# Attention over learned memories and a cosine feed-forward layer on one core: part-array products in longer pieces, and the whole turns of the cosine written as integers

## The chip, the cores and the metric

The kernel runs on one core of a Trainium2 chip. The metric is the device time of one execution in microseconds (us). Before the change the median of three runs is 718.47 us (717.94 to 719.61). A core has five engines that work side by side, each with its own queue of instructions: PE (TensorE, matrix products, results into PSUM), DVE (VectorE), ACT (ScalarE), POOL (GpSimd) and SP (which here issues most of the loads and stores). PE's weight loads are shown as an engine of their own, PEld.

## The reference

Eight batches of eight heads, 576 tokens, head size 64, 32 memories per head; then a feed-forward layer with 512 inputs and 2048 hidden units.

```python
a = phi - np.max(phi, axis=2, keepdims=True)
a = np.exp(a)
a = a / (np.sum(a, axis=2, keepdims=True) + 1e-09)
k_m = np.einsum('bhsm,bhsd->bhmd', a, k)
v_m = np.einsum('bhsm,bhsd->bhmd', a, v)
scores = scale * np.matmul(q, k_m.transpose(0, 1, 3, 2))
...
attn = attn / (np.sum(attn, axis=-1, keepdims=True) + 1e-09)
attn_out = np.matmul(attn, v_m)
...
h = x @ w_in          # x is attn_out, 4608 tokens x 512
g = h * np.cos(h)
return g @ w_out
```

Per batch and head, softmax weights over the tokens build 32 memory keys and values; each token then attends to the 32 memories, and the result goes through the layer with `h * cos(h)`. Weights arrive as 8-byte numbers and are brought to float32 and then to pairs of float16 (a high part and a rest) on the chip.

## The kernel before

**Two kinds of work.** The main loop runs over `12 * 16` units: twelve groups of 384 tokens (`grp`), each with sixteen slices of 128 hidden units (`f`). One unit is a first GEMM into a PSUM bank `hp` (`gemm1`, L500; in float32 for group 0, L491), the cosine on ACT and DVE (`act`, `act_end`), and a second GEMM that adds into three output accumulators (`gemm2`, L544; L539 for group 0). The second GEMM runs four units behind (`LAG`). A group of 384 tokens is two thirds of a batch or two halves: groups 1, 4, 7 and 10 hold the end of one batch and the beginning of the next, so `regions` gives two regions of 192 columns, the others one of 384.

**The cosine of a unit** (`act`, L505; `act_end`, L518). ACT writes `u = hp * c + 0.25`, the angle in turns (L509, once for each region); DVE casts `u` to integers `ni` (L514, the cast rounds) and subtracts them (L515); ACT takes the sine of 2 pi u (L519), which is the cosine of h; DVE multiplies it with `hp` (L523; L521 in group 0); ACT and DVE split the product into two float16 parts (L525, L526). The integers lie in the buffer `gp` that later takes the product (six buffers); `u` has three.

**The fold.** The attention's last product and the first GEMM are folded: `v_m` is multiplied into `w_in` first. For each batch `b`, a quarter `q` of the hidden units and each half `g` of the heads, `fold_psum` (L428) fills one PSUM bank `pv`, and `split_fold` (L443) brings it to two float16 parts `vw` on ACT (L445) and DVE (L446). For batch 1 the products are float32 on half of PE's columns (L433); from batch 2 on they are eight float16 products, each on a quarter of the columns (L439, shown as 128*32). Batch 0 has its own path (`fold_first`, L462).

**Preparing a batch** (`prep`: `memory`, L222, then `attend`, L331) is a generator. It yields after each small step: the softmax over tokens; the k/v products (L254, 40 products in float32 on a quarter of the columns, in five chunks of tokens; one yield after each chunk) into one bank `psA`; the division and transposes; the score products (L356, float32 on half of the columns, in three blocks of 256, 256 and 64 tokens, each into its own bank, with a DVE transpose after each, L358); softmax over memories; and the float16 parts of the weights. The k/v yields stand in this loop:

```python
for c, (s0, n) in enumerate(TCH):
    for g in range(2):
        for j in range(4):
            h = 4 * g + j
            nc.tensor.matmul(psA[32 * j:32 * (j + 1), g * KV:(g + 1) * KV],
                             lhsT=a[:n, c, h * M:(h + 1) * M], rhs=kvs[c][:n, h * KV:(h + 1) * KV],
                             start=(c == 0 and g == 0), stop=(c == 4), skip_group_check=True)
    yield
```

**The order of the work.** The main loop calls a batch's steps in a stretch of units (`jobs`), at the pace of `NSTEP = 24` steps over the stretch, and issues the folds at fixed units (`folds`): one half `(q, g)` every two units. Loads of the next batch are issued by steps of the one before (`load_phi`, `load_kv` after the k/v products, `load_q` after the scores). The order written in the program is a priority: a planner orders each engine's queue from it, from its own estimates of durations and from when buffers come free, so that instructions can be issued earlier or later than they are written; only a few are pinned (`keep_in_program_order`). On the chip each queue is then worked off in that order.

**PSUM.** Eight banks: three output accumulators, three for `hp`, and a pool of two (`ps_s`, `small_ps`) that folds, k/v products, transposes and scores share.

Of the kernel before, what the change touches and what calls it, by code (L numbers as in the profile page):

```python
# [22 lines left out]
P = 128  # L23
# [12 lines left out]
BLK = [(0, 256), (256, 256), (512, 64)]  # L36
BLK_FIRST = [(0, 256), (256, GT - 256), (GT, S - GT)]
TWO_PI_BELOW = 6.283185
EXP_MASK = 0x7F800000
NT = 4  # L40
LAG = 4
# [3 lines left out]
def attention_then_ffn(ctx: ExitStack, tc: tile.TileContext, phi, phiT, kv, qT, w_in, w_out, eye, out):  # L45
# [9 lines left out]
    def small_ps(name):  # L55
        return ps_s.tile([P, 512], F32, tag="ps_s", name=name)
# [5 lines left out]
    nc.vector.memset(vmask, 0.0)  # L62
    for j in range(4):
        nc.vector.memset(vmask[32 * j:32 * (j + 1), :, (j + 1) % 2], 1.0)

    w_in_sb = const.tile([P, NP, DF], F32, name="w_in_sb")

# [153 lines left out]
    def memory(b):  # L221
        a = loads.pop(("phi", b))  # L222
        if b < NT:

            nmx = wk.tile([P, 2], F32, tag="nmx", name=f"nmx_{b}", bufs=1)
            nc.vector.tensor_reduce(out=nmx, in_=loads.pop(("phiT", b)), op=ALU.max, axis=AX.X)
            top = small_ps(f"top_{b}")[:, 0:HM]
            for g in range(2):
                nc.tensor.matmul(top[:, g * P:(g + 1) * P], lhsT=nmx[:, g:g + 1].broadcast_to([P, P]), rhs=ident,
                                 start=True, stop=True)  # L230
        else:
            top = st["top", b]
        yield
        if b >= NT:
            yield
            yield
        for c0, c1, n in ((0, 2, P), (2, 4, P), (4, 5, S - 512)) if b == 0 else ((0, 4, P), (4, 5, S - 512)):
            ins = nc.vector.tensor_tensor(out=a[:n, c0:c1], in0=a[:n, c0:c1],
                                          in1=top[:n].unsqueeze(1).broadcast_to([n, c1 - c0, HM]),
                                          op=ALU.subtract)  # L240
            if b >= NT:

                tc.keep_in_program_order(ins)
            nc.scalar.activation(a[:n, c0:c1], a[:n, c0:c1], AF.Exp)  # L244
        yield
        if b:
            yield
        kvs = loads.pop(("kv", b))
        psA = small_ps(f"psA_{b}")
# [4 lines that stand above are left out]
                    nc.tensor.matmul(  # L254
                        psA[32 * j:32 * (j + 1), g * KV:(g + 1) * KV],
                        lhsT=a[:n, c, h * M:(h + 1) * M], rhs=kvs[c][:n, h * KV:(h + 1) * KV],
                        start=(c == 0 and g == 0), stop=(c == 4), skip_group_check=True)
            yield
        if b >= 1 and b + 1 < B and b + 1 != 2:
            load_phi(b + 1)  # L260
            load_kv(b + 1)
        pv = psA[:, 0:2 * KV].rearrange("p (g x) -> p g x", g=2)
        den = wk.tile([P, 2], F32, tag="den", name=f"den_{b}")
        nc.vector.tensor_scalar(out=den, in0=pv[:, :, 2 * D], scalar1=1e-9, scalar2=None, op0=ALU.add)
        nc.vector.reciprocal(out=den, in_=den)
        X = wk.tile([P, 2, P], F32, tag="X", name=f"X_{b}", bufs=1)
        for g in range(2):
            nc.vector.tensor_scalar(out=X[:, g], in0=pv[:, g, 0:2 * D], scalar1=den[:, g:g + 1], scalar2=None,
                                    op0=ALU.mult)
        if b:  # L270
            yield
        tpx = small_ps(f"tpx_{b}")
        for g in range(2):
            nc.tensor.matmul(tpx[:, g * P:(g + 1) * P], lhsT=X[:, g], rhs=ident, start=True, stop=True)
        km = wk.tile([P, NP, 2 * M], F32, tag="km", name=f"km_{b}", bufs=1)
        vm = wk.tile([P, NP, 2 * M], F32, tag="vm", name=f"vm_{b}")
        nc.gpsimd.memset(km, 0.0)
        nc.gpsimd.memset(vm, 0.0)
        tv = tpx[:, 0:HM].rearrange("p (c t m) -> p c t m", t=2, m=M)
        lo, hi = slice(0, D), slice(D, P)  # L280
        nc.scalar.mul(km[lo, :, 0:M], tv[lo, :, 0], 1.0 / math.sqrt(D))
        nc.scalar.mul(km[hi, :, M:2 * M], tv[hi, :, 1], 1.0 / math.sqrt(D))
        nc.vector.tensor_copy(out=vm[hi, :, 0:M], in_=tv[hi, :, 0])
        nc.vector.tensor_copy(out=vm[lo, :, M:2 * M], in_=tv[lo, :, 1])
        st["km", b], st["vm", b] = km, vm
        yield
        l1 = wk.tile([P, 4], F32, tag="l1", name=f"l1_{b}")
        nc.vector.tensor_reduce(out=l1, in_=X.rearrange("p g (t d) -> p (g t) d", t=2), op=ALU.add, axis=AX.X,
                                apply_absolute_value=True)
        nc.vector.tensor_tensor(out=l1, in0=l1, in1=vmask.rearrange("p g t -> p (g t)"), op=ALU.mult)  # L290
        l2 = wk.tile([P, 1], F32, tag="l2", name=f"l2_{b}")
        nc.vector.tensor_reduce(out=l2, in_=l1, op=ALU.max, axis=AX.X)
        l3 = wk.tile([P, 1], F32, tag="l3", name=f"l3_{b}")
        nc.gpsimd.partition_all_reduce(l3, l2, channels=P, reduce_op=RED.max)
        st["l3", b] = l3
        v_scale(b)
        yield
# [33 lines left out]
    def attend(b):  # L331
# [16 lines left out]
            flatp = at[:, r.start * M:r.stop * M]  # L348
            return flatp, flatp.rearrange("p (x m) -> p x m", m=M), r, r.stop - r.start

        def scores(i):
            t0, n = BL[i]
            sc = small_ps(f"sc_{b}_{t0}")
            for g in range(2):
                for p in range(2):
                    nc.tensor.matmul(sc[D * p:D * (p + 1), g * n:(g + 1) * n], lhsT=km[:, 2 * g + p],  # L356
                                     rhs=qt[:, 2 * g + p, t0:t0 + n], start=True, stop=True)
            nc.vector.transpose(at[:, 2 * t0:2 * (t0 + n)], sc[:, :2 * n])  # L358

        def shift(blocks):  # L360
            _, v, r, n = piece(blocks)
# [26 lines left out]
        if b == 0:  # L388
# [10 lines left out]
                    back(i)  # L399
                yield  # L400
            return
        for i in range(3):
            scores(i)
            yield
        if b >= 1 and b + 1 < B and b + 1 != 2:
            load_q(b + 1)
        pieces = ((0,), (1, 2))
# [38 lines left out]
        nc.vector.scalar_tensor_tensor(out=vw[:, 1, g], in0=src, scalar=T, in1=vw[:, 0, g],  # L446
                                       op0=ALU.mult, op1=ALU.subtract)

    def fold(b, q, g):
        if g == 0:  # L450
            st["vw", b, q] = wk.tile([P, 2, 2, FS], F16, tag="vw", name=f"vw_{b}_{q}", bufs=8)
        split_fold(b, st["vw", b, q], g, fold_psum(b, q, g))

    def fold_first(j):
        q, r = divmod(j, 2)
# [21 lines left out]
    def regions(grp):  # L477
        pair, r = divmod(grp, 3)
        b0 = 2 * pair
        if r == 0:  # L480
            return [(b0, 0, 0, GT)]
        if r == 1:
            return [(b0, GT, 0, S - GT), (b0 + 1, 0, S - GT, S - GT)]
        return [(b0 + 1, S - GT, 0, GT)]
# [20 lines left out]
    def act(grp, f, hp, pin=False):  # L505
        u = ew.tile([P, GT], F32, tag="u", name=f"u_{grp}_{f}", bufs=3)
        gp = ew.tile([P, GT], F32, tag="gp", name=f"gp_{grp}_{f}", bufs=6)
        for b, t0, c0, n in regions(grp):
            ins = nc.scalar.activation(u[:, c0:c0 + n], hp[:, c0:c0 + n], AF.Copy,  # L509
                                       scale=st["cu", b] if grp else 1.0 / (2.0 * math.pi), bias=0.25)  # L510
            if pin:
                tc.keep_in_program_order(ins)
        ni = gp.bitcast(I32)
        nc.vector.tensor_copy(out=ni, in_=u)  # L514
        nc.vector.tensor_tensor(out=u, in0=u, in1=ni, op=ALU.subtract)  # L515
        return u, gp

    def act_end(grp, f, hp, u, gp):  # L518
        nc.scalar.activation(u, u, AF.Sin, scale=TWO_PI_BELOW)  # L519
        if grp == 0:  # L520
            nc.vector.tensor_tensor(out=gp, in0=hp[:, :GT], in1=u, op=ALU.mult)  # L521
            return grp, f, gp
        nc.vector.scalar_tensor_tensor(out=u, in0=hp[:, :GT], scalar=2.0 ** -17, in1=u, op0=ALU.mult, op1=ALU.mult)  # L523
        gp = gp.bitcast(F16).rearrange("p (w x) -> p w x", w=2)
        nc.scalar.copy(gp[:, 0], u)  # L525
        nc.vector.tensor_tensor(out=gp[:, 1], in0=u, in1=gp[:, 0], op=ALU.subtract)  # L526
        return grp, f, gp
# [131 lines left out]
    for b in range(1, B):  # L659
        use = 48 * (b // 2) + 16 * (b % 2)  # L660
        before, length = {1: (5, 10), 2: (5, 13), 3: (6, 16)}.get(b, (6, 17) if b % 2 else (13, 18))
        jobs.append((b, use - before - length, use - before - 1))
        for q in range(NQ):
            for g in range(2):
                folds.setdefault(use - before + 4 * q + 2 * g, []).append((b, q, g))
    gens = {}
    pending, begun = [], []
    for i in range(12 * NF):
# [19 lines left out]
            pending.append(act_end(*begun.pop(0)))  # L688
        if len(pending) > LAG:
            gemm2(*pending.pop(0))  # L690
        for b, q, g in folds.get(i, ()):
            if q == g == 0:
                scales(b)
            fold(b, q, g)
        if i % 48 in (8, 24) and i > 8:
            out_scales(2 * (i // 48) + (i % 48 == 24))
        for b, s, e in jobs:
# [57 lines left out]
```

## Time and profile before

| | before |
|---|---|
| median of 3 runs | 718.47 us (717.94 to 719.61) |
| profiled execution, span from first to last instruction | 718.6 us |
| PE busy | 696.1 us (97%), 4578 matmuls |
| DVE busy | 570.4 us (79%), 1257 instructions |
| ACT busy | 521.5 us (73%), 965 instructions |
| mean granted clock of PE | 0.988 |

The profiled execution's span, 718.6 us, stands 0.1 us above the median of the runs. In the page, a group's row gives the line, engine, operation, output and inputs, shapes and count, then the busy time in us, the mean of one in ns, and the idle time of that engine just before, with what ended it. A matmul's shape 128*32 means 128 rows and 32 columns of the array. `issue` as a releaser means that the engine waited for nothing that the profile shows. Matmuls are pipelined, so their own lengths overlap; start-to-start distances tell what each costs.

### The profile page before, as it was taken

The page shows a single profiled execution, that of the slowest core. Times are in us where ns is not written, and L with a number is a line of the kernel's source. Part 1 is how long each engine was busy: PE and PEld are TensorE (multiplying, and loading weights), DVE is VectorE, ACT ScalarE, POOL GpSimd, SP SyncE. Part 2 cuts the span into 40 slices and gives each one's busy share as a digit, 9 for nine tenths or more (in the row PEclk, how much of TensorE's full clock was granted, in tenths as well). Part 3 has the DMA queues.
Part 4 walks back from the last instruction along what each step waited for, and adds up shares of the span by engine and source line. Part 5 has one row for each costly group of instructions (what it writes and reads, how often), then busy time and mean ns, then how long its engine had stood idle before and what let it go on. Part 6 is the DMA issues. An engine that isn't in the chain of part 4 may idle for free.

```text
span 718.6 us, 12024 instructions
## 1 busy us (share of the span) xinstructions
PE 696.1 (97%) x4578; PEld 357.7 (50%) x4578; DVE 570.4 (79%) x1257; ACT 521.5 (73%) x965; POOL 14.1 (2%) x34
## 2 busy tenths in 40 slices
PE   7689999999999999999999999999999999999997
PEld 3344445455445444666444444565444544555553
DVE  2778999998998997679876897679776987676764
ACT  1689999899887875678767696678767785665652
POOL 0000000000000000000000100000000000000000
PEclk9699999999999999999999999999999999999999
DMA  9994891525505300152103310152100000100101
GB/s 291 378 326 155 278 325 42 133 60 152 163 21 167 110 1 1 45 166 67 45 1 119 90 69 1 45 167 68 44 1 1 17 29 1 45 1 1 45 0 45
DMA packets 32233, 66.78 MB, mean 93 GB/s; under 512 B 2224, under 2 KB 12336, under 8 KB 32176
## 3 DMA queue, kind: packets, MB, share of 16 engines
q1 hardware_dynamic: 27712, 58.02, 25.1%
q10 hardware_dynamic: 4464, 8.00, 2.9%
q8 instruction: 36, 0.59, 0.4%
q14 instruction: 21, 0.17, 0.1%
HBM read 52.38 MB, written 9.44 MB: 86 GB/s over the span
## 4 chain that ended last, share of the span: by engine, by line
PE 65%; ACT 16%; DVE 13%; DMA 3%; issue 2%; SPq 1%; POOL 0%; ACTq 0%; DVEq 0%
PE acc L544 37%; PE hp L500 19%; PE pv L439 3%; ACT u L519 2%; ACT u L509 2%; DVE u L515 2%; DVE u L523 2%; PE sc L356 2%; DVE gp L526 2%; PE psA L254 2%; ACT L519 1%; DMA kv<-in_kv 1%; ACT L244 1%; DVE gp L514 1%; ACT vw L445 1%
## 5 line engine op out<-in xcount | busy, mean ns | idle before, releaser
L544 PE MATMUL acc<-wo,gp 128*128 128x512 f16 x1584 | 371.2, 379 | 0.0
L544 PEld LDWEIGHTS <-gp 128*128 128x128 f16 x1584 | 153.4, 98 | 161.5 <-issue 2.6
L500 PE MATMUL hp<-aT,vw 128*128 128x192 f16 (+1 forms) x1440 | 202.6, 284 | 0.3 <-DVE u L523 0.2
L500 PEld LDWEIGHTS <-vw 128*128 128x128 f16 x1440 | 125.0, 98 | 81.5 <-issue 29.0
L519 ACT ACTIVATE u<-u 128x384 f32<-128x384 f32 x192 | 100.2, 525 | 85.0 <-DVE u L515 84.1
L523 DVE SCALAR_TENSOR_TENSOR u<-hp,u 128x384 f32<-128x384 f32 x176 | 97.0, 553 | 45.7 <-ACT u L519 43.4
L509 ACT ACTIVATE u<-hp,cu 128x192 f32<-128x192 f32 (+1 forms) x240 | 110.7, 493 | 19.5 <-PE hp L500 11.9
L526 DVE TENSOR_TENSOR gp<-u,gp 128x384 f16<-128x384 f32 x176 | 96.7, 552 | 29.8 <-ACT gp L525 29.3
L525 ACT CAST gp<-u 128x384 f16<-128x384 f32 x176 | 89.2, 510 | 39.3 <-DVE u L523 37.1
L515 DVE TENSOR_TENSOR u<-u,gp 128x384 f32<-128x384 f32 x192 | 105.8, 553 | 3.2
L514 DVE CAST gp<-u 128x384 int32<-128x384 f32 x192 | 67.5, 353 | 21.6 <-ACT u L509 20.0
L539 PE MATMUL acc<-wo,gp 128*128 128x512 f32 x96 | 45.5, 603 | 1.6 <-DVE gp L521 1.6
L446 DVE SCALAR_TENSOR_TENSOR vw<-pv,vw 128x512 f16<-128x512 f32 x48 | 33.1, 689 | 4.2 <-ACT vw L445 3.0
L445 ACT ACTIVATE vw<-pv 128x512 f16<-128x512 f32 x48 | 28.4, 591 | 6.2 <-PE pv L439 5.4
L491 PE MATMUL hp<-aT,vf 128*128 128x384 f32 x64 | 26.5, 546 | 4.7 <-DVE gp L521 2.0
L519 ACT ACT_TABLE_LOAD x23 | 29.5, 1283 | 0.4
L539 PEld LDWEIGHTS acc<-wo,gp 128*128 128x128 f32 x96 | 17.0, 190 | 20.6 <-issue 14.7
L254 PE MATMUL psA<-kv,phi 128*32 128x129 f32 (+1 forms) x640 | 24.0, 280 | 3.2 <-DMA kv<-in_kv 1.8
L568 ACT ACTIVATE ob<-acc,os 128x512 f32<-128x512 f32 x27 | 17.9, 684 | 7.5 <-PE acc L544 5.6
L254 PEld LDWEIGHTS psA<-kv,phi 128*32 128x32 f32 (+1 forms) x640 | 16.3, 110 | 13.8 <-issue 7.4
L491 PEld LDWEIGHTS hp<-aT,vf 128*128 128x128 f32 x64 | 12.5, 207 | 18.2 <-DVE gp L521 4.6
L356 PE MATMUL sc<-q,km 128*64 128x256 f32 (+3 forms) x192 | 20.1, 337 | 0.0
(128 smaller groups left out, 555.5 us busy)
## 6 DMA issues: line engine op xcount, KB each, us to landing
kv<-in_kv SPq DMA_DIRECT2D x32, 516.0 KB, 5.6
raw_out<-in_w_out SPq DMA_DIRECT2D x8, 1024.0 KB, 4.9
q<-in_qT SPq DMA_DIRECT2D x7, 1152.0 KB, 5.5
out<-ob ACTq DMA_DIRECT2D x30, 256.0 KB, 2.1
raw_in<-in_w_in SPq DMA_DIRECT2D x6, 1024.0 KB, 7.9
phi<-in_phi SPq DMA_DIRECT2D x8, 512.0 KB, 6.7
w_in_sb<-w_in_parts SPq DMA_DIRECT2D x12, 256.0 KB, 4.4
phiT<-in_phiT SPq DMA_DIRECT2D x4, 576.0 KB, 6.4
```

The source lines that it names most:

```text
L254: nc.tensor.matmul(psA[32 * j:32 * (j + 1), g * KV:(g + 1) * KV], lhsT=a[:n, c, h * M:(h + 1) * M], rhs=kvs[c][:n, h * KV:(h + 1) * KV], s ...
L491: nc.tensor.matmul(hp[:, :GT], lhsT=st["vf", q][:, g, fo * P:(fo + 1) * P], rhs=st["aTf"][:, g], start=(g == 0), stop=(g == 1))
L500: nc.tensor.matmul(hp[:, c0:c0 + n], lhsT=vw[:, wi, g, fo * P:(fo + 1) * P], rhs=aT[:, ai, g, c1:c1 + n], start=(k == 0), stop=(k == 5))
L509: ins = nc.scalar.activation(u[:, c0:c0 + n], hp[:, c0:c0 + n], AF.Copy, scale=st["cu", b] if grp else 1.0 / (2.0 * math.pi), bias=0.25)
L514: nc.vector.tensor_copy(out=ni, in_=u)
L515: nc.vector.tensor_tensor(out=u, in0=u, in1=ni, op=ALU.subtract)
L519: nc.scalar.activation(u, u, AF.Sin, scale=TWO_PI_BELOW)
L523: nc.vector.scalar_tensor_tensor(out=u, in0=hp[:, :GT], scalar=2.0 ** -17, in1=u, op0=ALU.mult, op1=ALU.mult)
L525: nc.scalar.copy(gp[:, 0], u)
L526: nc.vector.tensor_tensor(out=gp[:, 1], in0=u, in1=gp[:, 0], op=ALU.subtract)
L539: nc.tensor.matmul(accs[grp][t], lhsT=gp[:, t * P:(t + 1) * P], rhs=wo[:, f + 1], start=(f == 0), stop=(f == NF - 1))
L544: nc.tensor.matmul(accs[grp][t], lhsT=gp[:, gi, t * P:(t + 1) * P], rhs=parts[:, wi], start=(f == 0 and gi == 0 and wi == 0), stop=(f == N ...
```

## The change

- `memory`: for batches after the first, the yield after each of the five k/v chunks is dropped; one yield follows after all five.
- `attend`: for batches after the first, the products of score blocks 0 and 1 are issued one after the other, into two banks, before the transposes of both; block 2 follows as before. Two yields instead of three.
- `fold`: both halves `g` are issued in one call. Products first, for both banks, then the splits. In the main loop a fold of a quarter stands at one unit (`4 * q + 1`) instead of two (`4 * q` and `4 * q + 2`).
- `act`: ACT writes `hp * c + 0.25` straight into the integer tile `ni` (its write rounds); DVE then computes `hp * c - ni` in one instruction from PSUM, once for each region. The cast is gone. The quarter turn, which the subtraction no longer holds, goes to the sine as a bias of pi/2 from a constant tile.

```diff
+    quarter = const.tile([P, 1], F32, name="quarter")
+    nc.vector.memset(quarter, HALF_PI_BELOW)
...
                         lhsT=a[:n, c, h * M:(h + 1) * M], rhs=kvs[c][:n, h * KV:(h + 1) * KV],
                         start=(c == 0 and g == 0), stop=(c == 4), skip_group_check=True)
+            if b == 0:
+                yield
+        if b:
             yield
...
-        for i in range(3):
-            scores(i)
-            yield
+        score_products(0)
+        score_products(1)
+        score_back(0)
+        score_back(1)
+        yield
+        score_products(2)
+        score_back(2)
+        yield
...
-    def fold(b, q, g):
-        if g == 0:
-            st["vw", b, q] = wk.tile([P, 2, 2, FS], F16, tag="vw", name=f"vw_{b}_{q}", bufs=8)
-        split_fold(b, st["vw", b, q], g, fold_psum(b, q, g))
+    def fold(b, q):
+        vw = wk.tile([P, 2, 2, FS], F16, tag="vw", name=f"vw_{b}_{q}", bufs=8)
+        st["vw", b, q] = vw
+        for g, pv in enumerate([fold_psum(b, q, g) for g in range(2)]):
+            split_fold(b, vw, g, pv)
...
+        ni = gp.bitcast(I32)
         for b, t0, c0, n in regions(grp):
-            ins = nc.scalar.activation(u[:, c0:c0 + n], hp[:, c0:c0 + n], AF.Copy,
-                                       scale=st["cu", b] if grp else 1.0 / (2.0 * math.pi), bias=0.25)
+            c, cu = slice(c0, c0 + n), st["cu", b] if grp else 1.0 / (2.0 * math.pi)
+            ins = nc.scalar.activation(ni[:, c], hp[:, c], AF.Copy, scale=cu, bias=0.25)
             if pin:
                 tc.keep_in_program_order(ins)
-        ni = gp.bitcast(I32)
-        nc.vector.tensor_copy(out=ni, in_=u)
-        nc.vector.tensor_tensor(out=u, in0=u, in1=ni, op=ALU.subtract)
+            nc.vector.scalar_tensor_tensor(out=u[:, c], in0=hp[:, c], scalar=cu, in1=ni[:, c],
+                                           op0=ALU.mult, op1=ALU.subtract)
...
-        nc.scalar.activation(u, u, AF.Sin, scale=TWO_PI_BELOW)
+        nc.scalar.activation(u, u, AF.Sin, scale=TWO_PI_BELOW, bias=quarter)
...
-            for g in range(2):
-                folds.setdefault(use - before + 4 * q + 2 * g, []).append((b, q, g))
+            folds.setdefault(use - before + 4 * q + 1, []).append((b, q))
```

`score_products(i)` and `score_back(i)` are the two halves of the old `scores(i)`: its four products, and its DVE transpose.

More of the change, by code (lines that the diff above doesn't have):

```diff
@@ L38 @@
 TWO_PI_BELOW = 6.283185
+HALF_PI_BELOW = 1.5707962
 EXP_MASK = 0x7F800000
@@ L349, in piece, with score_products @@
             return flatp, flatp.rearrange("p (x m) -> p x m", m=M), r, r.stop - r.start
-        def scores(i):
+        sc_at = {}
+        def score_products(i):
             t0, n = BL[i]
-            sc = small_ps(f"sc_{b}_{t0}")
+            sc_at[i] = sc = small_ps(f"sc_{b}_{t0}")
             for g in range(2):
@@ L357, in scores, with score_back @@
                                      rhs=qt[:, 2 * g + p, t0:t0 + n], start=True, stop=True)
-            nc.vector.transpose(at[:, 2 * t0:2 * (t0 + n)], sc[:, :2 * n])
+        def score_back(i):
+            t0, n = BL[i]
+            nc.vector.transpose(at[:, 2 * t0:2 * (t0 + n)], sc_at[i][:, :2 * n])
+        def scores(i):
+            score_products(i)
+            score_back(i)
         def shift(blocks):
@@ L690, in attention_then_ffn @@
             gemm2(*pending.pop(0))
-        for b, q, g in folds.get(i, ()):
-            if q == g == 0:
+        for b, q in folds.get(i, ()):
+            if q == 0:
                 scales(b)
-            fold(b, q, g)
+            fold(b, q)
         if i % 48 in (8, 24) and i > 8:
```

## Prediction

> **What bounds the kernel now.** I read the page's engine totals first, then busy time by stretch, then TensorE's timeline around the products that the change regroups, then the waits.
>
> ```profile
> PE 696.1 (97%) x4578; PEld 357.7 (50%) x4578; DVE 570.4 (79%) x1257; ACT 521.5 (73%) x965; POOL 14.1 (2%) x34
> ...
> PEclk9699999999999999999999999999999999999999
> ```
>
> ```profile
> 72.00:108.00 36.00, 34.36 (x117) 15.34 (x118) 34.38 (x73) 35.94 (x52) 0.91 (x3) 1.00 0.88 303
> 108.00:144.00 36.00, 36.00 (x188) 17.87 (x187) 35.16 (x76) 33.24 (x69) 0.35 (x1) 1.00 0.32 85
> 144.00:180.00 36.00, 35.66 (x294) 20.84 (x294) 33.16 (x65) 33.30 (x64) 0.31 (x1) 1.00 0.41 108
> 180.00:714.00 534.00, 532.64 (x3640) 275.65 (x3639) 419.54 (x947) 370.90 (x716) 10.53 (x19) 1.00 0.16 51
> ```
>
> The columns of the second are the stretch, its length, then PE, weight loads, DVE, ACT, POOL, the clock, the DMA share. From 108 us to 714 PE is busy for 604.3 of 606 us, at full clock. DVE is idle for 114 of the last 534 us, ACT for 163. So PE sets the end from 108 us on, and there only less PE time makes the kernel shorter. Before that, ACT is full (35.94 of 36) and DVE nearly.
>
> A busy PE isn't a streaming PE, though. This is its timeline around one fold of batch 4 (start, length, engine, line):
>
> ```profile
> 431.66 2.11 PE L544 MATMUL acc<-wo,gp 128*128 128x512 f16 x9
> 433.60 1.14 PE L500 MATMUL hp<-aT,vw 128*128 128x384 f16 x6
> 434.57 2.10 PE L544 MATMUL acc<-wo,gp 128*128 128x512 f16 x9
> 436.61 0.40 PE L439 MATMUL pv<-w_in,vp 128*32 128x512 f16 x4
> 436.84 0.39 PE L439 MATMUL pv<-w_in,vl 128*32 128x512 f16 x4
> 437.16 1.15 PE L500 MATMUL hp<-aT,vw 128*128 128x384 f16 x6
> ```
>
> Nine full-array matmuls followed by full-array ones take 433.60 - 431.66 = 1.94 us, or 0.216 each. Followed by products on a quarter of the columns (128*32) they take 436.61 - 434.57 = 2.04: **0.10 us going in**. The four `vp` products run side by side in 0.23 us (436.84 - 436.61), the four `vl` ones in 0.32 before a full-array matmul starts: **0.09 us coming out**. With 0.01 more on the first matmul after it, a trip out of the full array and back costs about 0.20 us beside its work. The waits view shows the trips at the weight loads:
>
> ```profile
> PEld L500 <- issue: 29.0, 79, 0.8
> PEld L439 <- issue: 19.7, 47, 0.4
> ...
> PEld psA L254 <- issue: 7.4, 18, 1.1
> ...
> PEld sc L356 <- issue: 4.4, 11, 0.6
> ...
> PEld pv L433 <- issue: 2.2, 5, 0.8
> ```
>
> (Columns: idle us in total, times, longest.) Some 80 trips, 47 of them folds, each with weight loads standing still for 0.42 us (19.7 / 47).
>
> **The change part by part: the products on TensorE.** No product is added or removed; 80 trips become fewer.
>
> *Folds of batches 2 to 7.* `fold` now issues both column halves (16 products) together: 4 times 6 pieces in place of the 47 trips seen. 23 trips at 0.20 = **4.6 us**. *Folds of batch 1* (L433, float32, on half the columns): 8 pieces become 4. No row shows two together; the price lies between the fold's 0.20 and the score's 0.26 (below). I take 0.25, nearer to the score, which is float32 on half the columns too: 4 times 0.25 = **1.0 us**.
>
> ```profile
> 384.07 0.65 PE L254 MATMUL psA<-kv,phi 128*32 128x129 f32 x16
> 384.65 0.60 PE L544 MATMUL acc<-wo,gp 128*128 128x512 f16 x2
> ...
> 385.63 1.05 PE L254 MATMUL psA<-kv,phi 128*32 128x129 f32 x32
> 386.61 1.15 PE L500 MATMUL hp<-aT,vw 128*128 128x384 f16 x6
> ...
> 404.31 1.95 PE L356 MATMUL sc<-q,km 128*64 128x256 f32 x16
> 406.19 1.15 PE L500 MATMUL hp<-aT,vw 128*128 128x384 f16 x6
> ...
> 327.06 1.08 PE L356 MATMUL sc<-q,km 128*64 128x256 f32 x8
> 328.08 1.16 PE L500 MATMUL hp<-aT,vw 128*128 128x192 f16 x12
> ```
>
> *k/v products.* A chunk alone (x16) takes 0.58 us from its start to the next full-array matmul, two chunks 0.98: the second adds 0.40, so each separate piece costs up to 0.18 and the 0.10 of entry, 0.28; the fold's trip, 0.20, is the lower bound. I take 0.24, the middle. Of the 18 trips I give 5 to batch 0, whose loop still yields chunk by chunk. The other 13 become 6 (batch 1's chunks are limited by other things, in the first 60 us): 7 times 0.24 = **1.7 us**.
>
> *Scores.* Two blocks together take 1.88 us (batch 5 already has them so), one alone 1.02: 2 x 1.02 - 1.88 = 0.16, and the entry makes 0.26. Batches 3, 5 and 7 already run blocks 0 and 1 back to back by the timeline. Four batches are left: **1.0 us**.
>
> Together 8.3 us. All but the scores of batch 1 lie after 98 us, nearly all where PE has no idle time to absorb the gain.
>
> **The cosine.** Per unit ACT still has one Copy pass, one sine and one cast, and DVE loses an instruction:
>
> ```profile
> L514 DVE CAST gp<-u 128x384 int32<-128x384 f32 x192 | 67.5, 353 | 21.6 <-ACT u L509 20.0
> ...
> L515 DVE TENSOR_TENSOR u<-u,gp 128x384 f32<-128x384 f32 x192 | 105.8, 553 | 3.2
> L523 DVE SCALAR_TENSOR_TENSOR u<-hp,u 128x384 f32<-128x384 f32 x176 | 97.0, 553 | 45.7 <-ACT u L519 43.4
> L446 DVE SCALAR_TENSOR_TENSOR vw<-pv,vw 128x512 f16<-128x512 f32 x48 | 33.1, 689 | 4.2 <-ACT vw L445 3.0
> ...
> L446 DVE SCALAR_TENSOR_TENSOR vw<-pv,T,vw 128x512 f16<-128x512 f32 x8 | 5.9, 743 | 0.2 <-ACT vw L445 0.2
> ```
>
> The new subtraction reads `hp` from PSUM as L523 does (553 ns at 384 columns) and, outside group 0, takes its factor from a tile, which costs 743 - 689 = 54 ns at L446: 607. From 384 to 512 columns a column costs (689 - 553) / 128 = 1.06 ns, so a half of 192 takes 403. Per unit 353 + 553 = 906 ns become 553 in group 0 (16 units), 607 in groups of one region (112), 806 in groups of two (64): 5.6 + 33.5 + 6.4 = 45.5 us less of DVE. While PE is full that is worth nothing to the end (cover: PE itself, 604.3 of 606 us). It is worth something only where PE waits for this chain:
>
> ```profile
> PE hp L491 <- DVE gp L521: 2.0, 1, 2.0
> ...
> PE acc L539 <- DVE gp L521: 1.6, 1, 1.6
> ```
>
> These are two waits in group 0, 3.6 us in all. The chain before each is shorter by one cast of 0.35; I take 0.4 us for both (bounds 0 and 3.6).
>
> ACT now writes int32, which no row of it shows. Nearest rows:
>
> ```profile
> L141 ACT ACTIVATE wo<-raw_out 128x1024 int16<-128x1024 uint8 x8 | 11.0, 1378 | 0.0
> ...
> L145 ACT ACTIVATE raw_out<-raw_out 128x1024 f32<-128x1024 f32 x8 | 9.3, 1168 | 0.0
> ```
>
> An integer write with an integer, strided read costs 0.21 us more per 1024 columns, or 0.08 per unit of 384: at most 192 x 0.08 = 15 us of ACT, under its 163 idle us after 180; in the full stretch 72 to 108 at most some 8 units, 0.6 us. The sine's bias from a tile costs the same kind of thing (L446's 54 ns is the nearest row). A write could also be no dearer at all; I take 0.3 us of loss for both.
>
> **What is moved.** A batch's preparation has five steps fewer but is still paced for 24, so it ends early; the loads of `phi`, `kv` (4 steps) and `q` (5) are issued to SP's queue sooner, into tiles whose readers are done by the same order as before. DMA runs at a share of 0.16 there, so nothing. `ni` is now written by ACT straight into `gp`, whose buffer (six) is released by the second GEMM six units back, ahead of this unit's first GEMM on PE: no new wait unless the planner swaps those.
>
> **Sum.** 8.3 + 0.4 - 0.3 = 8.4, and 0.2 off for small new waits below: the profiled execution's span is 718.6 us, 0.1 above the median of the runs (718.47), so nothing lies around it, and the forecast is **710.4 us**.
>
> **Rivals.**
>
> *Two banks at once (slower).* The small PSUM pool has two banks. A fold now needs both, and so does a pair of score blocks. While the next batch's preparation holds one (k/v sums, transposes, scores), PE stands in order at the fold's second half until an evacuation ends:
>
> ```profile
> L445 ACT ACTIVATE vw<-pv 128x512 f16<-128x512 f32 x48 | 28.4, 591 | 6.2 <-PE pv L439 5.4
> ```
>
> 591 on ACT and 689 on DVE (L446): 1.28 us. About half of the 28 folds run beside a preparation: 14 x 1.28 = 18 us, so 718.6 - 8.4 + 18 = 728. It decides from 8.4 / 28 = 0.3 us per fold. Against it: PE has hardly waited at folds so far (the 47 trips account for L439's idle weight loads), and the planner gives a PE slot to other work when a bank isn't free. The Trainium skill speaks for it: TensorEngine Tiling (Array Packing), "PSUM Bottleneck", holds that packing speeds up TensorE but not the emptying of PSUM, which may become the limit. By that rule the time would be this rival's; the trace so far doesn't show it. Chance 0.11.
>
> *The planner doesn't keep the pieces together.* It already splits a piece that the program issues as one; this is one fold half of batch 1:
>
> ```profile
> 133.21 1.07 PE L433 MATMUL pv<-w_in_sb,vm 128*64 128x512 f32 x2
> ...
> 135.61 1.07 PE L433 MATMUL pv<-w_in_sb,vm 128*64 128x512 f32 x2
> ```
>
> Where the second bank is late it would issue the second half later. Half the gain: 718.6 - 4.2 = 714.4. Chance 0.12.
>
> *ACT and DVE take turns on a bank.* In groups of two regions (64 units) the DVE subtraction of the first region and ACT's pass over the second read the same `hp` bank. In the trace two such readers don't overlap, though neither needs the other's result:
>
> ```profile
> L561 DVE TENSOR_SCALAR ob<-acc,os 128x256 f32<-128x256 f32 x1 | 0.5, 484 | 0.4 <-ACT ob L560 0.4
> ```
>
> So ACT pass, DVE, ACT pass, DVE: 0.40 us of ACT waiting per unit unless other work fills it. In group 1 (about 112 to 165 us), where ACT has 5.5 us idle in 72 and DVE 3.7, 16 x 0.40 = 6.4 us would be lost: 718.6 - 8.4 + 6.4 = 716.6. The weight splits queued there are such filling, so chance 0.06. (The Trainium skill, PSUM — Partial Sum Buffer, "PSUM bank collisions raise a hardware error", says that two engines may not touch one bank and quadrant at once, reads included; the trace agrees by the 0.4 us above.)
>
> *No change:* the trips go but the time is spent elsewhere, 718.5. PE's 604 of 606 us speak against it: 0.05.
>
> **How the numbers follow.** Forecast 0.66. A change under 0.2% (1.4 us) can't be told from none here. Faster: 0.66 + 0.12 and most of the third rival, 0.82; same 0.07; slower 0.11. The low end takes all 3.6 us of group 0's waits: 718.6 - 8.3 - 3.6 = 706.7, little likely, so 707.0. The high end takes in the planner's rival and the turn-taking one: 716.8. Left out are the slower case, no change and a little more, about 0.19.
>
> **What would show it.** Right: the waits at L439's weight loads fall from 47 to about 24 and at L500's from 79 to under 50; the timeline shows folds of 16 with one entry; the cast is gone and DVE busy near 525 us; PE still full from 108 us on. Wrong: PE idle before L439 that ends with DVE at L446 (the first rival), folds still of 8 (the second), ACT idle at L509 ended by DVE's new subtraction with PE idle beside it in 112 to 165 us (the third).

## The result and the profile after

The changed kernel takes 712.11 us (median of 4 runs, 711.6 to 714.09) against 718.76 us before on the same chip: a ratio of 0.9913, 95% interval 0.989 to 0.9935. In a later session it took 713.26 us against 718.47 (0.9929, 0.9897 to 0.9961). The forecast was 710.4 us, the range 707.0 to 716.8. The profiled execution, the longest of the four, has a span of 712.3 us and a time of 714.09: 1.8 us lie around the span.

The page's totals of the changed kernel, and three of its stretches (columns as in the prediction):

```profile
PE 686.4 (96%) x4578; PEld 364.3 (51%) x4578; DVE 532.4 (75%) x1132; ACT 518.7 (73%) x951; POOL 13.7 (2%) x34
```

```profile
108.00:144.00 36.00, 35.20 (x198) 19.08 (x196) 35.71 (x78) 33.91 (x70) 0.35 (x1) 1.00 0.32 81
144.00:180.00 36.00, 35.49 (x300) 21.35 (x299) 35.13 (x78) 31.18 (x63) 0.67 (x2) 1.00 0.46 127
180.00:708.00 528.00, 524.01 (x3624) 279.91 (x3622) 381.02 (x817) 367.13 (x701) 9.68 (x18) 1.00 0.15 51
```

PE is still the engine that sets the end, but it is no longer quite full: 4.0 us idle in the last 528, where before it was 1.4 in 534. DVE has 38 us less to do.

One fold, and the k/v products of one batch, in PE's timeline after the change:

```profile
348.33 2.11 PE L566 MATMUL acc<-wo,gp 128*128 128x512 f16 x9
350.36 0.40 PE L460 MATMUL pv<-w_in,vp 128*32 128x512 f16 x4
350.59 0.39 PE L460 MATMUL pv<-w_in,vl 128*32 128x512 f16 x4
350.80 0.39 PE L460 MATMUL pv<-w_in,vp 128*32 128x512 f16 x4
351.02 0.39 PE L460 MATMUL pv<-w_in,vl 128*32 128x512 f16 x4
351.34 1.15 PE L522 MATMUL hp<-aT,vw 128*128 128x384 f16 x6
...
381.28 2.54 PE L258 MATMUL psA<-kv,phi 128*32 128x129 f32 x80
383.75 1.47 PE L566 MATMUL acc<-wo,gp 128*128 128x512 f16 x6
```

All sixteen fold products run with one way in (350.36 - 348.33 = 2.03, where nine full-array matmuls need 1.94) and one way out; from `vl` to the next `vp` there is no gap (0.21). All 40 k/v products of a batch run as one stretch of 2.47 us (80 records: a float32 product has two). The waits at PE's weight loads show how many trips are left:

```profile
PEld L522 <- issue: 17.9, 40, 1.2
...
PEld L460 <- issue: 10.3, 25, 0.4
```

47 fold trips became 25, and 79 returns to the first GEMM became 40, as the prediction had it (24, and under 50).

**One account for all kernels.** From the start times of all matmuls after 100 us PE's time was divided in three. Streaming: full-array matmuls at their usual distance (0.216 us for 512 columns in float16, 0.163 for 384, and so on). Part-array stretches: from the last full-array matmul's usual end to the next one's start, so with the way in and out; each stretch is one trip. Waits: what a step is longer than its kind ever is without a wait. The columns on trips, part-array time and waits carry the argument; streaming is the same work everywhere (536 to 541 us, by how much of it falls ahead of 100 us).

The account is that of the one execution that was profiled, the medians are those of all runs. Two profiles lie at an end of their runs: "fold halves apart" was the shortest of ten executions, "products alone, folds one unit later" the longest of four. The split between part-array time and waits is an estimate. The waits view, which lists only longer waits, gives less everywhere but much the same order: 1.3 us before, 4.5 to 5.1 for the changed kernel, 6.0 with its folds later, 6.4 with DVE loaded, 8.6 to 11.4 for the products alone. (Some of the expectations below were written with an earlier count: 6.4 and 12.9 us of waits, 5.2 us for 25 trips.)

| kernel | median, us | ratio to before, 95% | trips | part-array, us | PE waits, us |
|---|---|---|---|---|---|
| before | 718.4 to 718.8 | | 84 | 72.4 | 3.4 |
| changed | 712.11 | 0.9913 (0.989 to 0.9935) | 46 | 62.2 | 6.9 |
| changed, again | 713.26 | 0.9929 (0.9897 to 0.9961) | 46 | 62.2 | 6.5 |
| cosine alone | 718.63 | 0.9999 (0.9986 to 1.0013) | 82 | 72.1 | 3.5 |
| products alone | 725.41 | 1.0093 (1.0072 to 1.0115) | 52 | 64.6 | 14.0 |
| products alone, folds one unit later | 726.05 | 1.0109 (1.0056 to 1.0161) | 51 | 64.8 | 17.5 |
| products alone, folds one unit sooner | 722.10 | 1.0039 (1.002 to 1.0057) | 47 | 63.2 | 12.7 |
| changed, folds one unit later | 714.49 | 0.9948 (0.9922 to 0.9973) | 47 | 63.1 | 8.6 |
| changed, one full-array product in each fold | 716.82 | 0.9981 (0.9968 to 0.9994) | 71 | 67.6 | 4.2 |
| changed, score blocks apart | 716.75 | 0.9974 (0.9958 to 0.999) | 51 | 64.4 | 6.7 |
| changed, fold halves apart | 718.24 | 0.9997 (0.9982 to 1.0012) | 67 | 67.9 | 5.5 |
| changed, DVE loaded off the chain | 717.54 | 0.9993 (0.9975 to 1.001) | 47 | 63.0 | 8.6 |
| changed, steps spread | 720.21 | 1.0029 (1.0007 to 1.005) | 47 | 64.9 | 10.8 |
| changed, three small banks | 724.34 | 1.0081 (1.0056 to 1.0106) | 48 | 64.9 | 12.1 |

So the change took 38 trips and 10.2 us of part-array time out of PE's queue after 100 us and put 3.1 to 3.5 us of new waits into it: 6.7 to 7.1 us less. The spans of the two profiles differ by 6.3 us, the medians by 5.2 to 6.7. About 1.1 of the 10.2 us are no gain: half a fold of batch 1 now runs ahead of 100 us (96.75 us, both halves together; before, the halves ran at 98.10 and 101.89).

### The profile page after: what moved, and what is told of

Read it like the earlier page. It is cut to its first block, busy times and chain, and to the rows that moved or that the text cites. A ratio compares the mean times of both kernels' runs of the same rounds, so it can differ in the third digit from the quotient of the medians.

```text
span 712.3 us, 11782 instructions
## 1 busy us (share of the span) xinstructions
PE 686.4 (96%) x4578; PEld 364.3 (51%) x4578; DVE 532.4 (75%) x1132; ACT 518.7 (73%) x951; POOL 13.7 (2%) x34
## 4 chain that ended last, share of the span: by engine, by line
PE 63%; DVE 18%; ACT 15%; DMA 2%; issue 1%; SPq 0%; ACTq 0%; DVEq 0%
PE acc L566 35%; PE hp L522 17%; DVE u L536 3%; ACT u L541 3%; DVE u L545 3%; DVE gp L548 2%; PE psA L258 2%; PE hp L513 2%; PE sc L365 2%; DVE vw L467 2%; PE pv L460 2%; ACT gp L547 2%; DVE wo L189 2%; DMA kv<-in_kv 1%; DVE w_in_parts L200 1%
## 5 line engine op out<-in xcount | busy, mean ns | idle before, releaser
L522 PEld LDWEIGHTS <-vw 128*128 128x128 f16 x1440 | 128.3, 98 | 77.6 <-issue 17.9
L541 ACT ACTIVATE u<-u,quarter 128x384 f32<-128x384 f32 x192 | 117.0, 616 | 64.5 <-DVE u L536 63.6
L533 ACT ACTIVATE gp<-hp,cu 128x192 int32<-128x192 f32 (+1 forms) x240 | 115.3, 492 | 27.9 <-PE hp L522 11.8
L536 DVE SCALAR_TENSOR_TENSOR u<-hp,cu,gp 128x192 f32<-128x192 f32 (+1 forms) x240 | 119.0, 504 | 21.9 <-ACT gp L533 21.5
L513 PE MATMUL hp<-aT,vf 128*128 128x384 f32 x64 | 28.2, 579 | 7.3 <-DVE vf L486 3.1
L467 DVE SCALAR_TENSOR_TENSOR vw<-pv,vw 128x512 f16<-128x512 f32 x48 | 31.5, 685 | 3.0 <-ACT vw L466 2.9
L466 ACT ACTIVATE vw<-pv 128x512 f16<-128x512 f32 x48 | 26.8, 588 | 1.1 <-PE pv L460 0.9
L258 PE MATMUL psA<-kv,phi 128*32 128x129 f32 (+1 forms) x640 | 21.0, 275 | 3.2 <-DMA kv<-in_kv 1.8
L365 PEld LDWEIGHTS sc<-q,km 128*64 128x64 f32 x192 | 12.1, 140 | 12.6 <-issue 4.4
```

The lines of the kernel that those rows point to most:

```text
L513: nc.tensor.matmul(hp[:, :GT], lhsT=st["vf", q][:, g, fo * P:(fo + 1) * P], rhs=st["aTf"][:, g], start=(g == 0), stop=(g == 1))
L522: nc.tensor.matmul(hp[:, c0:c0 + n], lhsT=vw[:, wi, g, fo * P:(fo + 1) * P], rhs=aT[:, ai, g, c1:c1 + n], start=(k == 0), stop=(k == 5))
L533: ins = nc.scalar.activation(ni[:, c], hp[:, c], AF.Copy, scale=cu, bias=0.25)
L536: nc.vector.scalar_tensor_tensor(out=u[:, c], in0=hp[:, c], scalar=cu, in1=ni[:, c], op0=ALU.mult, op1=ALU.subtract)
L541: nc.scalar.activation(u, u, AF.Sin, scale=TWO_PI_BELOW, bias=quarter)
```

## The experiments

**The two halves of the change alone.** Products alone: the changed kernel with `act` and `act_end` of before. Cosine alone: the kernel before with `act` and `act_end` of the changed one.

> The changed kernel with the old cosine: folds, k/v products and scores in longer pieces, the cast and the subtraction from SBUF as before. If the gain is the trips in and out of the full array (about 33 fewer at 0.20 to 0.26 us, 8.3 us, less the new waits of some 3.7 us that the changed kernel's timeline shows), it keeps the gain: 711 to 714 us. If the gain came from DVE's 38 us of freed time, most of it is lost: 716 to 719.

> The kernel before with the new cosine alone; all pieces short. If trips on a full PE are the gain, DVE's freed time is worth nothing to the end: 717.5 to 719.5 us, with DVE busy about 38 us less and PE's trips as before (about 80). If the shorter chain is the gain: 712 to 715.

Measured: 725.41 and 718.63 us. Neither theory holds for both runs. The cosine alone is worth nothing, as the trips theory said; but the products alone are 0.9% **slower** than before, although the trips are gone (52 of 84, 64.6 us). The waits take more than that: 14.0 us. Together the two halves are 0.9% faster. The waits view of the products alone, with ACT's wait for the subtraction in the first line:

```profile
ACT u L541 <- DVE u L537: 92.2, 98, 1.8
...
PE acc L566 <- ACT ob L590: 2.8, 7, 0.6
PE psA L258 <- ACT phi L248: 2.5, 4, 1.8
```

And of the changed kernel:

```profile
ACT u L541 <- DVE u L536: 63.6, 94, 2.5
...
PE sc L365 <- DVE vw L467: 1.7, 1, 1.7
PE hp L522 <- DVE u L545: 1.1, 2, 0.9
PE acc L566 <- DVE ob L578: 0.7, 1, 0.7
```

With the old cosine ACT stands 92 us for DVE ahead of its sines. That wait alone does no harm: the kernel before has 84.1 us of it, with 3.4 us of waits on PE. It is with the longer pieces that other work of ACT comes late for PE, the evacuation of the output accumulators (`ob`, partly on DVE) and the exponentials that the k/v products need (`phi`): by the waits view 5.3 of 9.2 us here, 5.3 of 11.4 and 3.4 of 8.6 in the two other plans below, 1.9 of 5.1 in the changed kernel. That the wait ahead of the sine is what makes them late is argued, not shown.

**Was it one unlucky plan?** The planner orders every queue anew for each variant, so a single slow variant proves little. The products alone were built twice more, with each fold one unit later and one sooner, and the changed kernel with each fold one unit later:

```diff
-            folds.setdefault(use - before + 4 * q + 1, []).append((b, q))
+            folds.setdefault(use - before + 4 * q + 2, []).append((b, q))
```

> The changed kernel itself once more, on the chip and beside the runs of the three variants here. 711 to 713.5 us; its PE waits after 100 us 6 to 8 us, as in its first profile, if the waits belong to the program and not to the execution.

> The changed kernel with each fold one unit later (4q + 2 in place of 4q + 1): nothing in work, trips or banks changes, only where the planner puts things. If the waits follow from DVE's load and the cosine's chain, they stay near 7 us and the time at 711 to 714. If they are mostly a matter of how this one plan falls, they move by some us either way: anything from 709 to 719.

> The longer pieces with the old cosine (725.4 us, 14 us of waits on PE after 100 us), each fold one unit later. If the old cosine's cast is what makes longer pieces wait, it stays slow: 721 to 727, 11 us of waits or more. If that plan was unlucky, the waits fall to 5 to 8 us: 713 to 718.

> The same with each fold one unit sooner (4q). As for the one before: 721 to 727 with 11 us of waits or more if the old cosine is the cause, 713 to 718 if one plan was unlucky.

Measured: 713.26, 714.49, 726.05 and 722.10 us. Three plans with the old cosine have 12.7 to 17.5 us of waits, two with the new one 6.5 to 8.6. The plan moves the waits by 2 to 5 us; the cosine by 4 at the least and some 7 in the mean. The table loads on ACT, which the planner also moves, don't explain it: the products alone and the changed kernel with its folds later both have 42 of them, with 14.0 and 8.6 us of waits, and the kernel before has 46. Between the two profiled executions of the changed kernel the waits differ by 0.4 us, so they belong to the program.

**DVE's load or the chain?**

```diff
+        nc.vector.tensor_reduce(out=spare, in_=gp[:, 0:GT // 2], op=ALU.max, axis=AX.X)
         return u, gp
```

The added maximum goes to a cell that nothing reads.

> The changed kernel with one more DVE instruction per unit, off the cosine's chain: a maximum over 192 columns of the integers, into a cell that nothing reads (some 0.34 us by the rows of reductions, 192 units, 65 us of DVE; the cast that the change took away had 67.5). The products alone were slower (725.4) with 12.9 us of waits on PE after 100 us, the changed kernel has 6.4. If it is DVE's load that makes the longer pieces wait, the waits come back: 10 us or more of them, 716 to 722 us. If it was the cosine's chain of dependent instructions, or the plan alone, they don't: 711 to 714.

Measured: 717.54 us, 8.6 us of waits: between the two. The group and the waits view of this kernel:

```profile
L539 DVE TENSOR_REDUCE spare<-gp 128x1 f32<-128x192 f32 x192 | 65.7, 342 | 0.0
```

```profile
ACT u L543 <- DVE u L537: 58.3, 91, 2.2
```

DVE has at least as much to do as with the old cast (65.7 us in place of 67.5; busy for 579.1 us in all against 571.2 in the products alone), yet ACT's wait for the subtraction stays short (58.3; 92.2, 84.3 and 103.7 with the old cosine), and PE's waits rise by 1.7 to 2.1 us in place of 6 to 11. In time it costs 4 to 5 us by the medians, 1.9 between the spans of the profiles. Load is a part of it. That the rest is the dependent cast, between ACT's pass and its sine, agrees with ACT's wait, but no run changes the chain's length with DVE's load left as it is: it wasn't shown by itself.

**The price of a trip.**

```diff
+        if b >= 2 and g == 1:
+            w2 = st["w2", q]
+            nc.tensor.matmul(pv[:, 0:128], lhsT=w2[:, 0, 0, 0:P], rhs=w2[:, 1, 0, 0:P], start=True, stop=True)
```

> The changed kernel with one full-array product of 128 columns put between the two halves of each fold of batches 2 to 7 (its result is overwritten by the second half, so nothing of the computation changes). 24 trips come back without any change of steps, banks or evacuations. At 0.20 us a trip and 0.06 us for streaming 128 columns: 24 x 0.26 = 6.2 us, so about 718. If a trip isn't what costs, only the streaming: 24 x 0.06 = 1.4 us, so 713.5.

Measured: 716.82 us, 3.6 to 4.7 over the changed kernel. PE's timeline at the fold that was shown above:

```profile
349.89 0.40 PE L463 MATMUL pv<-w_in,vp 128*32 128x512 f16 x4
350.12 0.39 PE L463 MATMUL pv<-w_in,vl 128*32 128x512 f16 x4
350.44 0.23 PE L453 MATMUL pv<-w_in 128*128 128x128 f16 x1
350.60 0.40 PE L463 MATMUL pv<-w_in,vp 128*32 128x512 f16 x4
350.82 0.39 PE L463 MATMUL pv<-w_in,vl 128*32 128x512 f16 x4
351.15 1.15 PE L525 MATMUL hp<-aT,vw 128*128 128x384 f16 x6
```

From `vl` to the small product 0.32 us in place of 0.21, from there to `vp` 0.16 for 128 columns: 0.10 out and, with 0.06 for streaming 128 columns, 0.10 in. The fold takes 351.15 - 349.89 = 1.26 us against 0.98. Over the whole kernel 25 more trips make 67.6 - 62.2 = 5.4 us: **0.22 us a trip**. The waits happened to fall by 2.3 to 2.7 us in this plan, and so the time rose by less than the 6.2 expected. The trip is what costs.

**Where the new waits come from: scores apart, halves apart, spread steps, three banks.** In order: the loop `scores(i); yield` over the three blocks, as before; `fold(b, q, g)` for one half at `4 * q + 2 * g`, as before; the pace

```diff
-                want = math.ceil((i - s + 1) * NSTEP / (e - s + 1))
+                want = math.ceil((i - s + 1) * (17 if b < NT else 19) / (e - s + 1))
```

and `bufs=2` for the first GEMM's PSUM pool (`ps_h`), `bufs=3` for the small one (`ps_s`).

> The changed kernel with the three score blocks one by one again, as before (one bank each, three steps). If the two waits at the scores in the changed kernel (1.8 us at 397 us and 0.5 at 474) come from two banks being wanted at once beside a fold, they go, 2.3 us, and four trips come back, 4 x 0.26 = 1.0: about 710.8. If they have another source (evacuations of a fold that come late whoever waits), they stay and only the trips are paid: 713.1.

> The changed kernel with the fold's two halves apart again, each at its own unit; k/v products, scores and cosine as changed. The measured price of a trip, 0.207 us (5.2 us for the 25 trips of the product between halves), gives 25 to 28 trips, +5.5 us: 717.5. If the fold's two banks filled at once are what PE waits for (scores at 397 us waited 1.8 us for DVE's second evacuation, with the scores together or apart), some 2.5 us of waits go with it: 715.

> The changed kernel with the preparation paced for the steps it now has (17 for batches 1 to 3, 19 after) over the same stretch of units, in place of 24. If the waits come from preparation bunched into the first four fifths of its stretch, they fall from 6.4 us to about 3.2, as before the change: 709. If the bunching is harmless, 711.5 to 713.

> The changed kernel with three small PSUM banks and two for the first GEMM, in place of two and three. If PE's waits are for a small bank (scores and k/v sums after DVE's evacuation of a fold, about 2.7 us), they go: 709.5, provided that two banks are enough for the first GEMM. If the first GEMM needs its third bank, PE waits there for DVE's product with hp instead and the time goes up by microseconds: over 715.

Measured: 716.75, 718.24, 720.21 and 724.34 us.

*Scores apart* was expected at 710.8 or 713.1 and is slower than both. The large wait at the scores is still there (1.6 us, ahead of 401.05 us), so it doesn't need the pair of banks that the scores take; the small one at 474 us is gone, and another of 0.5 us has come. Five trips and 2.2 us of part-array time come back: four of scores, and one because the planner has cut a fold of batch 1 in two (1.1 us; more on that below). Between the two profiles the span grows by 2.8 us, 2.0 of it trips and waits and 0.7 work that had not been done by 100 us. That the medians lie further apart, 3.5 to 4.6 us, stays open. *Halves apart* gives the whole gain back: 21 trips and 5.7 us return, the waits fall by only 1 to 1.4.

*Three banks* do remove the waits at scores and k/v sums: the waits view after 100 us has 2.6 us of them in the changed kernel, none here. But with two banks for the first GEMM PE waits for the product with `hp`:

```profile
PE hp L522 <- DVE u L545: 5.6, 10, 1.6
```

A small bank is really what was missing at those places, and one from the first GEMM is worth more where it is.

*Spread steps* are worse: the scores of batch 3, right behind a fold, wait for 2.5 us and then run 1.35 us longer (below), which is 3.9 of the 6.6 us that trips and waits take more than in the changed kernel; a fold of batch 1 that is cut in two is another 1.1. So spreading the steps removed no waits here; whether the early end of a preparation helps by itself, one plan doesn't show.

## Why the prediction was right, and where it wasn't

**The bound and the trips: right.** PE set the end, and a trip costs 0.22 us (predicted 0.20 for folds, 0.24 to 0.26 for float32). The sum had 38 trips (23 + 4 + 7 + 4) and 8.3 us; after 100 us 38 trips and 10.2 us are gone. That the counts agree is luck. By what stands in each stretch, 18 are folds of batches 2 to 7 alone, 12 hold k/v products, 5 are folds of batch 1 and 3 scores: six of the 18 k/v stretches held a fold too, which the counts of idle weight loads don't tell. In us, folds of batches 2 to 7 and k/v products together gave 6.5 (forecast 6.3), the scores 0.8 (1.0; those of batch 1 lie ahead of 100 us), the folds of batch 1 2.9 (1.0). Of these 2.9, 1.1 are the half that moved ahead of 100 us, and 1.1 the fold half that the planner had cut in two, the second rival's lines:

```profile
133.21 1.07 PE L433 MATMUL pv<-w_in_sb,vm 128*64 128x512 f32 x2
134.21 1.47 PE L544 MATMUL acc<-wo,gp 128*128 128x512 f16 x6
...
142.92 1.08 PE L433 MATMUL pv<-w_in_sb,vm 128*64 128x512 f32 x4
143.93 0.26 PE L500 MATMUL hp<-aT,vw 128*128 128x192 f16 x1
```

Two records alone hold PE for 1.00 us (134.21 - 133.21), all four for 1.01 (143.93 - 142.92). So a piece that is cut in two costs its whole length once more, not a trip's 0.24, and the changed kernel no longer has that cut. Of the second rival itself little came: the planner kept all folds of batches 2 to 7 but one together (25 pieces, not 24).

**"0.2 off for small new waits": mis-sized.** They are 3.1 to 3.5 us. The first rival's mechanism is in the trace, at 397 us:

```profile
395.46 1.28 ACT L433 ACT_TABLE_LOAD   x1
...
396.75 0.63 ACT L433 ACTIVATE at<-at 128x512 f32<-128x512 f32 x1
...
397.69 1.07 ACT L466 ACTIVATE vw<-pv 128x512 f16<-128x512 f32 x2
...
398.49 1.28 DVE L467 SCALAR_TENSOR_TENSOR vw<-pv,vw 128x512 f16<-128x512 f32 x2
...
399.23 0.45 PE L365 MATMUL sc<-q,km 128*64 128x64 f32 x8 [1.75 <-DVE vw L467]
```

Both banks of a fold wait behind a table load and an exponential on ACT, are then evacuated one after the other, and PE stands 1.8 us at the scores behind them. It happens once at this length, not at 14 folds, so the rival's 18 us didn't come. By the waits view, 1.7 us of the new waits are this one; the others are shorter and of several kinds.

**"While PE is full that is worth nothing to the end": the step that failed.** It holds for the cosine alone (718.63 us). In the changed kernel it is worth 9 to 13 us: that much is lost when the longer pieces run with the old cosine. PE being full was taken as the cover; but PE is kept full by ACT and DVE being early, and with longer pieces and the old cosine they no longer were (the late `ob` and `phi` above). That the total came out near the forecast rests on both halves being there, and that is luck: from this prediction one would have expected 710 to 711 for the products alone, where 725.4 was measured.

**The prices of the cosine.** The changed kernel, with DVE's group first and the others in the order of the page's list:

```profile
L536 DVE SCALAR_TENSOR_TENSOR u<-hp,cu,gp 128x384 f32<-128x384 f32 x112 | 67.8, 611 | 11.0 <-ACT gp L533 10.8
L536 DVE SCALAR_TENSOR_TENSOR u<-hp,cu,gp 128x192 f32<-128x192 f32 x128 | 51.2, 410 | 11.0 <-ACT gp L533 10.7
```

```profile
L541 ACT ACTIVATE u<-u,quarter 128x384 f32<-128x384 f32 x192 | 117.0, 616 | 64.5 <-DVE u L536 63.6
...
L533 ACT ACTIVATE gp<-hp,cu 128x384 int32<-128x384 f32 x112 | 63.9, 577 | 9.5 <-PE hp L522 8.0 <-ACT ob L590 1.2
L533 ACT ACTIVATE gp<-hp,cu 128x192 int32<-128x192 f32 x128 | 51.5, 418 | 18.4 <-DVE u L536 11.8 <-PE hp L522 3.8 <-DVE wo L189 1.4
```

and of ACT in the kernel before:

```profile
L519 ACT ACTIVATE u<-u 128x384 f32<-128x384 f32 x192 | 100.2, 525 | 85.0 <-DVE u L515 84.1
...
L509 ACT ACTIVATE u<-hp,cu 128x384 f32<-128x384 f32 x112 | 63.8, 576 | 13.4 <-PE hp L500 9.1 <-ACT ob L568 1.7 <-DVE gp L526 0.6
L509 ACT ACTIVATE u<-hp,cu 128x192 f32<-128x192 f32 x128 | 47.1, 420 | 6.1 <-PE hp L500 2.9 <-issue 1.2 <-DVE gp L526 1.0
```

The new subtraction takes 611 and 410 ns (predicted 607 and 403). Writing integers costs ACT nothing (577 and 418 against 576 and 420). The sine's bias costs 91 ns (616 against 525) where 54 was taken. ACT's waits for DVE's new subtraction ahead of its pass over `hp`, the third rival, come to 11.8 us in all, but only 0.8 of them lie in group 1 (110 to 165 us), where the rival had 6.4, and PE's view there has no wait that they end. DVE is busy for 532 us (predicted 525). The rows of cast and subtraction did fall as forecast, from 173.3 us to 127.7 (67.8 + 51.2 + 8.7 for group 0), by 45.6; DVE's busy time, in which neighbours that overlap count once, fell by 38.0.

**The sum's base.** "Nothing lies around it" was wrong: time is 1.7 to 2.6 us more than the span in every later execution, and of 65 later spans of the kernel before (714.3 to 720.3 us) only three were longer than the 718.6 of the profiled execution, so that was a long one. The forecast's drop of 8.2 us is to be held against 6.3 between the two profiles and 5.2 to 6.7 between the medians. Trips worth somewhat more than forecast and new waits of 3.1 to 3.5 us in place of 0.2 offset each other in part; that much of the agreement is luck too.

## What to carry to other kernels

On a full PE, count how often the queue leaves the full array and comes back: that has a price of its own (0.22 us here) that hides inside PE's busy time, and joining pieces saves it. But a longer piece asks the other engines for more at once; before an instruction off the critical path is priced at nothing, ask how early its engine is now, and whether the other half of the same change uses that up. Test the halves apart and in more than one plan: here one half alone did nothing, the other alone did harm, and together they were faster.

## What the runs showed of the hardware that was not expected

**A PE wait of 2.5 us can cost more than itself.** The kernel with spread steps, PE's timeline (start, length) and two stretches with the granted clock in the third column from the right:

```profile
228.84 0.38 PE L566 MATMUL acc<-wo,gp 128*128 128x512 f16 x1
231.75 3.30 PE L365 MATMUL sc<-q,km 128*64 128x256 f32 x16 [2.53 <-issue]
234.98 1.25 PE L566 MATMUL acc<-wo,gp 128*128 128x512 f16 x5
```

```profile
229.00:235.00 6.00, 3.47 (x19) 1.95 (x18) 4.03 (x7) 2.92 (x7) 0.00 (x0) 0.72 0.01 1
231.80:234.40 2.60, 2.60 (x14) 1.66 (x16) 1.61 (x3) 0.70 (x2) 0.00 (x0) 0.50 0.01 3
```

The products of two score blocks (16 records), which took 1.88 us in the kernel before, take 234.98 - 231.75 = 3.23 after it, at a granted clock of 0.50 while they run. The changed kernel has the same in group 0: PE idle for 3.1 us before 78.1 us, a clock of 0.89 from 72 to 80:

```profile
78.13 4.22 PE L513 MATMUL hp<-aT,vf 128*128 128x384 f32 x7 [3.12 <-DVE vf L486]
```

```profile
72.00:80.00 8.00, 4.88 (x16) 1.99 (x15) 7.94 (x15) 7.97 (x13) 0.00 (x0) 0.89 0.81 258
```

The Trainium skill, TensorE: Matmul & The Clock Gate, "HAM oscillation — how this bites in real kernels", sets the limit at PE-idle gaps over some 3.4 us; here 2.5 us of idle time were enough. The length of the gap alone doesn't decide: in the products alone with folds one unit later 2.35 us were enough (a clock of 0.50 from 230.2 to 233.6 us), in the changed kernel with a full-array product in each fold 2.86 us were not:

```profile
76.99 2.20 PE L516 MATMUL hp<-aT,vf 128*128 128x384 f32 x6 [2.86 <-DVE vf L489]
```

```profile
77.00:80.50 3.50, 3.50 (x10) 2.00 (x11) 3.18 (x5) 3.50 (x7) 0.00 (x0) 1.00 0.93 369
```

**A bias from a tile costs the sine 91 ns.** The Trainium skill, ScalarE: Activation LUTs, "What ACT_TABLE_LOAD costs", gives about 93 ns for each operand that is read per partition; the trace agrees.
